# Step 0 of a linear-attention stage in banks of its own, its loads and the first unit after it moved, and settling products of another shape

## The chip, the cores and the metric

The kernel runs on one core of one Trainium2 chip. The metric is the device time of one execution in microseconds (us). Five engines run their own instruction queues side by side: PE (TensorE, matrix products into PSUM), DVE (VectorE), ACT (ScalarE), POOL (GpSimd) and SP (SyncE, which here issues every transfer). An instruction waits on semaphores for what it needs, and everything behind it on its engine waits with it.

## The reference

```python
def _attn_ref(r, k, v, w, u):               # (4, 8, 768, 48): batch, heads, time, width
    state = np.zeros((B, H, D, D))
    for t in range(S):
        kt, vt, rt = (k[:, :, t], v[:, :, t], r[:, :, t])
        cur = np.einsum('bhd,bhe->bhde', u[None] * kt, vt)
        y[:, :, t] = np.einsum('bhd,bhde->bhe', rt, state + cur)
        state = w[None, :, :, None] * state + np.einsum('bhd,bhe->bhde', kt, vt)

def _moe_ref(x, w_gate, w_val, w_out):      # 3072 tokens, 384 -> 1536 -> 384
    gate = 1.0 / (1.0 + np.exp(-(x @ w_gate)))
    return gate * (x @ w_val) @ w_out

def _moe2_ref(x, w_in, w_out):              # 384 -> 2048 -> 384
    h = np.maximum(x @ w_in, 0.0)
    return h * h @ w_out
```

The output is `_moe2_ref(_moe_ref(x))`, where x is y with batch and time as 3072 tokens and heads and width as 384 features.

## The kernel before

**Attention.** Time is cut into six steps of 128 positions (`NCH`), two halves of 64 each. A unit is one step of one of four batches: units 0 to 3 are step 0, units 4 to 7 step 1, and so on to 23. `load_unit` fetches a unit in four transfers (`kv`, `rn`, `kT`, `rT`, 1.1 MB). The recurrence is done in blocks: `attn_pre` (POOL) and `attn_sum` (DVE, into `dv`) give the diagonal of the scores, `attn_diag` (ACT, eight small activations) writes it into `am`; `attn_prep` (DVE) scales kT and rT by decay tables; `attn_scores` (PE) multiplies them into PSUM, and `attn_mask` (DVE) copies the scores under the mask into `am`. `attn_kh` (POOL) scales k, `attn_sums` (PE) makes each half's sum of k by v, and `attn_us` (ACT) copies it out. `attn_mid` and `attn_state` (DVE) carry the state on.

**A visit.** `attn_out(n)` is one visit of PE to attention: the masked scores of unit n by v, the first `reads` of the state, a `settle`, then scores and sums of unit n + 1, a `settle` ahead of and behind the sums, and the second `reads`. ACT then copies `us` of n + 1 and the results `ys`; two transfers (six after the fourth unit) put `ys` into `xraw`, the input x of the next stage. All PSUM of a visit is the tile `att`, three banks: outputs y1 and y2, scores `pa` and sums `pu` lie in halves of them. `settle` is a small product into an unused tile; it stands wherever the products behind it write, from another half of PE's rows, a bank that products ahead of it write.

**Hidden layers.** `phases` lists the stages of the two feed-forward networks: phase 0 is the first seven hidden units (`CUT`) of network 1 on step 0, the next phases are network 1 on steps 1 to 5, then the rest of step 0, then network 2. `inner(i, f, fill)` makes one hidden unit f: nine products `pg`, a sigmoid `s` (ACT), nine products `pv`, `s` times `pv` (DVE), its split into `gh` (ACT) and `gl` (POOL in phase 0, else DVE), and, one unit late, nine products of the projection (`finish`). Each operand is split into a high and a low part, so a product takes three passes.

**Weights.** `convert` turns 64-bit weights into such pairs as a pipeline over three calls: ACT and DVE on `raw`, DVE on the next, ACT (`wu`, high) and POOL (`wu`, low) on the one after. `load_raw` fetches a `raw` tile (0.4 MB), four deep.

**What sets the order.** The program is written in order by hand (`manual_schedule`), each engine taking its instructions in that order. In phase i the attention of step i + 1 is spread over slots, three for each hidden unit (`unit_ops`; `fill` runs a slot's operations, then one `convert`). `starts` says at which slot each unit's visit stands. `warm` puts filler products on PE. The tiles of a pool's tag rotate through `bufs` buffers.

In step 0 (line 631 on) the order of one round is `attn_pre`, `attn_prep` of unit n + 2, fillers, the visit n, `attn_sum(n + 2)`, `attn_mask(n + 1)`, `attn_mid`, `attn_state(n)`, then diagonals and `attn_kh` of n + 2. After the fourth round stand two conversions, 24 fillers and the split of x into `xh` (ACT) and `xl` (DVE).

## Time and profile before

| | us |
|---|---|
| median of three runs (989.1 to 991.38) | 990.55 |
| the profiled execution | 990.49 |
| its span, first to last instruction | 988.7 |
| PE busy in the span | 961.3 |
| DVE, ACT, POOL busy | 453.1, 401.8, 135.0 |
| mean granted clock of PE | 0.976 |

The page's slices cut the span into 40 equal parts of 24.7 us and give each engine's busy share in tenths; `PEclk` is the clock that PE was granted, in tenths of full speed (5 is 1.2 GHz, 9 is the full 2.4). The timeline lists instructions by start: start, length, engine, line, operation, result from operands, count, and in brackets how long the engine was idle before and what ended that. The window views give busy time of each engine, its count in brackets, then granted clock, the DMA engines' mean busy share and GB/s.

### The profile page before, as it was taken

Reading aid. Unit: us, or ns where it says so; the run is one execution under the profiler, and the core shown is the slowest. Engines: PE = TensorE matmul, PEld = TensorE weight load, DVE = VectorE, ACT = ScalarE, POOL = GpSimd, SP = SyncE. Lnnn points to the kernel's source line nnn. Section 1 sums busy time; section 2 is a strip of 40 time slices with the busy share of each in tenths; the row PEclk is TensorE's granted clock in tenths of the full one; section 3 lists DMA queues with packets and bytes.
Section 4 is the critical chain, followed back from the end, with each engine's and each line's share of the span. In section 5 each row is a group of like instructions: output and inputs, shape, how many; then the busy total and the mean of one; then the engine's idle time right before and its main releaser. Section 6 shows DMA issues by size and latency. Waiting matters only on the chain.

```text
span 988.7 us, 16639 instructions
## 1 busy us (share of the span) xinstructions
PE 961.3 (97%) x6904; PEld 764.3 (77%) x6904; DVE 453.1 (46%) x742; ACT 401.8 (41%) x826; POOL 135.0 (14%) x121
## 2 busy tenths in 40 slices
PE   6888899999999999999999999999999999999997
PEld 3566688888888888887888888888888888888886
DVE  5667757754434444422344465343333433433332
ACT  3656756533233223322366564232332322323322
POOL 6446735300000000000033121000000000000000
PEclk7679899999999999999999999999999999999999
DMA  8664555522122221100244440010100100100000
GB/s 302 203 211 126 169 167 161 147 79 84 52 60 89 90 67 27 68 7 15 95 128 123 154 155 1 1 64 1 33 32 1 64 1 1 65 1 1 32 0 33
DMA packets 42235, 76.86 MB, mean 78 GB/s; under 512 B 5168, under 2 KB 17584, under 8 KB 42160
## 3 DMA queue, kind: packets, MB, share of 16 engines
q1 hardware_dynamic: 42160, 75.80, 24.1%
q8 instruction: 54, 0.88, 0.4%
q14 instruction: 21, 0.17, 0.1%
HBM read 60.05 MB, written 11.01 MB: 72 GB/s over the span
## 4 chain that ended last, share of the span: by engine, by line
PE 90%; DVE 4%; ACT 2%; issue 1%; POOL 1%; DMA 1%; SPq 0%; DVEq 0%; ACTq 0%
PE pg L429 34%; PE two L448 16%; PE pv L429 14%; PE po L448 11%; PE att L448 7%; PE att L270 5%; PE pw L590 1%; PE tok L278 1%; DVE first L239 1%; DMA first<-in_rkv 1%; DVE am L319 1%; ACT am L255 1%; POOL wu L134 0%; DVE raw L156 0%; DVE mid L388 0%
## 5 line engine op out<-in xcount | busy, mean ns | idle before, releaser
L429 PE MATMUL pg<-xh,wu 128*128 128x512 f32 x1008 | 315.0, 397 | 5.8 <-ACT wu L133 3.7
L429 PEld LDWEIGHTS pg<-xh,wu 128*128 128x128 f32 x1008 | 189.8, 188 | 54.2 <-ACT wu L133 5.0
L429 PE MATMUL pg<-xl,wu 128*128 128x512 f32 x504 | 195.0, 395 | 0.0
L576 ACT CAST gh<-s 128x512 fp32r<-128x512 f32 (+1 forms) x169 | 104.9, 621 | 194.0 <-DVE s L572 120.6
L412 DVE TENSOR_TENSOR gl<-s,gh 128x512 fp32r<-128x512 f32 x162 | 113.3, 699 | 86.6 <-PE po L448 56.3
L575 DVE TENSOR_TENSOR s<-s 128x512 f32<-128x512 f32 (+1 forms) x97 | 66.6, 687 | 181.4 <-ACT s L574 181.4
L448 PE MATMUL two<-gh,wu 128*128 128x512 f32 x472 | 148.1, 395 | 0.0
L429 PE MATMUL pv<-xh,wu 128*128 128x512 f32 x432 | 141.2, 408 | 0.4 <-POOL wu L134 0.4
L574 ACT ACTIVATE s<-pg 128x512 f32<-128x512 f32 (+1 forms) x97 | 57.6, 594 | 190.3 <-PE pg L429 190.3
L572 DVE TENSOR_TENSOR s<-pv,s 128x512 f32<-128x512 f32 x72 | 49.6, 689 | 176.1 <-PE pv L429 172.6
L429 PEld LDWEIGHTS pg<-xl,wu 128*128 128x128 f32 x504 | 95.0, 189 | 22.7 <-DVE xl L412 0.3
L448 PEld LDWEIGHTS two<-gh,wu 128*128 128x128 f32 x472 | 89.3, 189 | 21.7
L448 PE MATMUL po<-gh,wu 128*128 128x512 f32 (+1 forms) x338 | 105.5, 392 | 0.0
L429 PEld LDWEIGHTS pv<-xh,wu 128*128 128x128 f32 x432 | 81.1, 191 | 21.0 <-POOL wu L134 0.8
L448 PE MATMUL two<-gl,wu 128*128 128x512 f32 x236 | 92.5, 392 | 0.0
L558 ACT ACTIVATE s<-pg 128x512 f32<-128x512 f32 x72 | 43.6, 606 | 110.5 <-PE pg L429 110.2
L429 PE MATMUL pv<-xl,wu 128*128 128x512 f32 x216 | 86.8, 402 | 0.0
L448 PEld LDWEIGHTS po<-gh,wu 128*128 128x128 f32 x338 | 63.4, 188 | 14.6
L154 ACT ACTIVATE raw<-raw 128x384 bf16<-128x384 bf16 x68 | 73.6, 1082 | 0.0
L448 PE MATMUL po<-gl,wu 128*128 128x512 f32 (+1 forms) x169 | 66.2, 392 | 0.0
L448 PE MATMUL att<-gh,wu 128*128 128x512 f32 (+1 forms) x204 | 63.4, 392 | 0.0
L255 ACT ACTIVATE am<-anti,dv 128x64 f32<-128x64 f32 x192 | 50.1, 340 | 16.5 <-DVE dv L245 16.5
(295 smaller groups left out, 919.6 us busy)
## 6 DMA issues: line engine op xcount, KB each, us to landing
raw<-in_w SPq DMA_DIRECT2D x68, 384.0 KB, 3.2
kv<-in_rkv SPq DMA_DIRECT2D x16, 384.0 KB, 3.3
xin<-x2d SPq DMA_DIRECT2D x6, 768.0 KB, 4.2
out<-x2s SPq DMA_DIRECT2D x18, 256.0 KB, 2.0
first<-in_rkv SPq DMA_DIRECT2D x16, 256.0 KB, 5.8
kT<-in_rkv SPq DMA_DIRECT2D x16, 256.0 KB, 4.5
rT<-in_rkv SPq DMA_DIRECT2D x16, 256.0 KB, 5.0
x2d<-x2s SPq DMA_DIRECT2D x15, 256.0 KB, 2.0
```

The source lines that it names most:

```text
L154: nc.scalar.activation(top, top, AF.Prelu, scale=2.0**-112, alpha=2.0**32)
L239: nc.vector.tensor_mul(t, t, two)
L255: nc.scalar.mul(am_t[n][:, h], anti, dv_t[n][:, h : h + 1])
L270: nc.tensor.matmul(out, lhsT=lhsT, rhs=rhs, start=(bank, q) not in opened, stop=True, skip_group_check=True)
L412: (eng or nc.vector).tensor_tensor(out=dst, in0=src, in1=high.bitcast(F32), op=ALU.subtract)
L429: nc.tensor.matmul(ps, lhsT=a, rhs=b_, start=(i == 0), stop=(i == len(pairs) - 1))
L448: nc.tensor.matmul(po[k][:, ts], lhsT=a, rhs=b_[:, ts], start=(first and m == 0), stop=(last and m == 2 and ts is cuts[-1]),)
L558: nc.scalar.activation(s, pg, AF.Sigmoid)
L572: nc.vector.tensor_tensor(out=s[:, ts], in0=pv[:, ts], in1=s[:, ts], op=ALU.mult)
L574: nc.scalar.activation(s[:, ts], pg[:, ts], AF.Relu)
L575: nc.vector.tensor_mul(s[:, ts], s[:, ts], s[:, ts])
L576: nc.scalar.copy(gh[:, ts], s[:, ts])
```

## The change

It has these parts. Scores of units 0 to 3 go to a tile `pa0` of two banks (tag `o`, used by the projection later), and stand ahead of the visit's other products instead of within it. In step 0 the state updates are left out of the rounds and done in `attn_mid` of step 1 (units 5 to 7, and unit 4), for which `us` gets five buffers. Unit 4's scores, sums and `us` stand behind the loop and not in visit 3; unit 5's preparation goes to the first three slots of phase 0. Transfers are put in another order, units 6 and later are fetched from visit 4 on. Table products stand ahead of the first scores. The visits of phase 0 stand at slots 3, 8, 12, 17 (were 0, 3, 9, 12), those of later phases at 0, 9, 18, 27 (were 0, 6, 15, 24). Fillers: 8, 2, 4, 4 and then 4 and 14, were 8, 6, 2, 2 and 24. `settle` loads 48 columns and not 8, so that its product has the shape of the others.

```diff
--- before.py
+++ after.py
@@ -67,7 +67,7 @@
     IN_W = 8
     CUT = 7
 
-    WARM0, WARM_OUT, WARM_X = 13, (8, 6, 2, 2), 24
+    WARM0, WARM_OUT, WARM_X = 13, (8, 2, 4, 4), (4, 14)
 
     anti = cp.tile([C, L], F32, name="anti")
     mask8 = cp.tile([C, L], U8, name="mask8")
@@ -102,6 +102,8 @@
             o += m
         for i in (2, 3, 0, 1):
             nc.sync.dma_start(out=got[i][0], in_=got[i][1])
+            if n == 0 and i == 3:
+                nc.sync.dma_start(out=u_bc, in_=u.to_broadcast([C, H * D]))
         k_t[n], r_t[n] = (t[0:DP].rearrange("p (j t) -> p j t", j=HP) for t, _ in got[:2])
         kv_t[n], rn_t[n] = got[2][0], got[3][0]
 
@@ -207,12 +209,12 @@
             nc.scalar.copy(th.rearrange("p (j r d) -> p j r d", j=HP, r=2)[:, :, par], pth)
 
 
-    am_t, dv_t = {}, {}
+    am_t, dv_t, pa_t = {}, {}, {}
     bank, us_t, mid_t = {}, {}, {}
 
 
     att = pp.tile([P, 3, 512], F32, name="att")
-    pa = att[:, 1:3, 0 : HP * L].rearrange("p r (j t) -> p r j t", j=HP)
+    pas = att[:, 1:3, 0 : HP * L].rearrange("p r (j t) -> p r j t", j=HP)
     y1, y2 = att[:, 0, 0 : HP * L], att[:, 2, HP * L :]
     PU = HP * L
     pu = [att[:, i, PU : PU + HP * D].rearrange("p (j d) -> p j d", j=HP) for i in (1, 0)]
@@ -275,19 +277,26 @@
     def settle(x):
 
         tok = pp.tile([P, T], F32, tag="v", name="tok")
-        nc.tensor.matmul(tok[0:8, 0:8], lhsT=x[0:D, 0:8], rhs=x[0:D, 0:8], start=True, stop=True)
+        nc.tensor.matmul(tok[0:D, 0:8], lhsT=x[0:D, 0:D], rhs=x[0:D, 0:8], start=True, stop=True)
 
     def attn_scores(n):
 
         if n >= NU:
             return
         k, r = k_t[n], r_t[n]
+        banks, pa_t[n] = (1, 2), pas
+        if n < B:
+
+            two = pp.tile([P, 2, T], F32, tag="o", name="pa0")
+            banks, pa_t[n] = (3, 4), two[:, :, 0 : HP * L].rearrange("p r (j t) -> p r j t", j=HP)
+            opened.difference_update([(m, q) for m in banks for q in range(2)])
+        pa = pa_t[n]
         for j in range(HP):
             for par in range(2):
                 x = slice(64 * par, 64 * par + D)
                 for a in range(2):
                     t = slice(a * L, (a + 1) * L)
-                    mm64(1 + par, a, pa[64 * a : 64 * a + L, par, j], k[x, j, t], r[x, j, t])
+                    mm64(banks[par], a, pa[64 * a : 64 * a + L, par, j], k[x, j, t], r[x, j, t])
 
 
     width = (64, D)
@@ -316,13 +325,13 @@
             return
         am = am_t[n].rearrange("p (j r) t -> p r j t", r=2)
         m = mask8.unsqueeze(1).unsqueeze(1).to_broadcast([C, 2, HP, L])
-        nc.vector.copy_predicated(am, m, pa)
+        nc.vector.copy_predicated(am, m, pa_t.pop(n))
 
     def attn_us(n):
 
         if n >= NU:
             return
-        us = us_t[n] = sp.tile([DP, 2, HP, D], F32, tag="us", name="us", bufs=2)
+        us = us_t[n] = sp.tile([DP, 2, HP, D], F32, tag="us", name="us", bufs=5)
         for a in range(1 if units[n][0] == NCH - 1 else 2):
             nc.scalar.copy(us[:, a], pu[a][0:DP])
         if units[n][0] == 0:
@@ -347,6 +356,8 @@
                         st = mid_t[n][o, j] if a else state[o, b, j]
                         mm(a, q, j, D, st, r_t[n][o, j, a * L : (a + 1) * L])
 
+        if n + 1 < B:
+            attn_scores(n + 1)
         for j in range(HP):
             for q in range(2):
                 h = head(q, j)
@@ -355,13 +366,16 @@
                     mm(a, q, j, width[q], kv[x, h * D :][:, : width[q]], am[x, h])
         reads(0)
         settle(kv)
-        attn_scores(n + 1)
-        attn_sums(n + 1)
+        if n >= B:
+            attn_scores(n + 1)
+        if n != B - 1:
+            attn_sums(n + 1)
         settle(kv)
         reads(1)
-        while len(kv_t) <= n + (4 if len(kv_t) < IN_W + 2 else 3) and len(kv_t) < NU:
+        while n >= B and len(kv_t) <= n + (4 if len(kv_t) < IN_W + 2 else 3) and len(kv_t) < NU:
             load_unit(len(kv_t))
-        attn_us(n + 1)
+        if n != B - 1:
+            attn_us(n + 1)
         if b == 0:
             bank["y"] = sp.tile([P, B, HP, C], F32, tag="ys", name="ys", bufs=1)
             xraw[c] = sp.tile([P, KT, B, C], F32, tag="xraw", name="xr", bufs=1)
@@ -383,6 +397,8 @@
 
         if n >= NU or units[n][0] == 0:
             return
+        if units[n][0] == 1:
+            attn_state(n - B)
         mid = mid_t[n] = sp.tile([DP, HP, D], F32, tag="mid", name="mid", bufs=2)
         nc.vector.tensor_mul(mid, state[:, units[n][1]], decay)
         nc.vector.tensor_add(mid, mid, us_t[n][:, 0])
@@ -457,8 +473,13 @@
 
     def unit_ops(c, tiles):
 
-        starts = [b * (tiles - 1) // B for b in range(B)] + [tiles - 1]
+
+        starts = (0, 9, 18, 27, 36) if tiles == F1 else (3, 8, 12, 17, 21)
         slots = [[] for _ in range(3 * tiles)]
+        if c == 1:
+            slots[0].append(lambda: (attn_pre(B + 1), attn_prep(B + 1)))
+            slots[1].append(lambda: (attn_kh(B + 1), attn_sum(B + 1)))
+            slots[2].append(lambda: (attn_diag(B + 1, 0), attn_diag(B + 1, 1)))
         for b in range(B):
             n = c * B + b
             ops = [
@@ -471,7 +492,7 @@
                 lambda n=n: attn_diag(n + 2, 1),
                 lambda n=n: attn_kh(n + 2),
             ]
-            s0, room = 3 * starts[b], 3 * (starts[b + 1] - starts[b])
+            s0, room = starts[b], starts[b + 1] - starts[b]
             for i, op in enumerate(ops):
                 slots[s0 + i * room // len(ops)].append(op)
         return slots
@@ -597,56 +618,72 @@
         nc.sync.dma_start(out=w_sb, in_=wt)
         id_sb = sp.tile([DP, D], F32, tag="ev", name="id_sb", bufs=2)
         maskf = sp.tile([C, L], F32, tag="ev", name="maskf", bufs=2)
+        nc.sync.dma_start(out=id_sb, in_=ident)
         load_unit(0)
-        nc.sync.dma_start(out=u_bc, in_=u.to_broadcast([C, H * D]))
         nc.sync.dma_start(out=anti, in_=antid)
         nc.sync.dma_start(out=maskf, in_=mask)
-        nc.sync.dma_start(out=id_sb, in_=ident)
         load_unit(1)
+        load_unit(2)
         load_raw(0)
+        load_unit(3)
         load_raw(1)
-        for n in range(2, B):
-            load_unit(n)
-            load_raw(n)
+        load_raw(2)
+        load_unit(4)
+        load_raw(3)
         powers = tables()
         attn_pre(0)
         nc.gpsimd.tensor_copy(mask8, maskf)
+        attn_pre(1)
         attn_prep(0)
+        state_tables(*powers)
+        attn_scores(0)
         attn_sum(0)
-        attn_pre(1)
         attn_diag(0, 0)
         attn_diag(0, 1)
-        attn_scores(0)
+        attn_kh(0)
+        attn_kh(1)
         attn_prep(1)
+        attn_mask(0)
         attn_sum(1)
-        state_tables(*powers)
-        attn_mask(0)
         attn_diag(1, 0)
-        attn_diag(1, 1)
-        attn_kh(0)
         attn_sums(0)
         attn_us(0)
-        attn_kh(1)
-        convert()
+        attn_diag(1, 1)
         for n in range(B):
-            attn_pre(n + 2)
-            attn_prep(n + 2)
+            m = n + 2
+            if m < B:
+                attn_pre(m)
+                attn_kh(m)
+                attn_prep(m)
             warm(WARM_OUT[n])
             attn_out(n)
-            attn_sum(n + 2)
-            attn_mask(n + 1)
-            attn_mid(n + 1)
-            attn_state(n)
-            attn_diag(n + 2, 0)
-            attn_diag(n + 2, 1)
-            attn_kh(n + 2)
-            if n == 0:
+            if m <= B:
+                attn_mask(n + 1)
+            if m < B:
+                attn_sum(m)
+                attn_diag(m, 0)
+                attn_diag(m, 1)
+            if n in (1, 2):
                 convert()
-        for _ in range(2):
-            convert()
-        warm(WARM_X)
+
+        load_unit(B + 1)
+        attn_pre(B)
+        attn_kh(B)
+        attn_prep(B)
+        attn_sum(B)
+        attn_diag(B, 0)
+        attn_diag(B, 1)
+        warm(WARM_X[0])
+        attn_scores(B)
+        attn_sums(B)
+        attn_us(B)
+        convert()
+        convert()
+        warm(WARM_X[1])
         for k in range(KT):
             x_from(0, k)
+        attn_mask(B)
+        attn_mid(B)
         for i, (layer, c, f0, f1) in enumerate(phases):
             ops = unit_ops(i + 1, f1 - f0) if i + 1 < NCH else []
             slot = 0
```

On DVE, in step 0, between the first diagonals and the first conversion. `dv` is a unit's diagonal, `am` its score tile, `first` a loaded piece, `us`, `wdec` and `state` belong to the recurrence. Before:

```order
L245 TENSOR_REDUCE dv_361<-first_89 128x8
L319 COPY_PREDICATED am_239<-mask8_70,att_110 128x2x4x64
L397 TENSOR_TENSOR state_77<-us_267,wdec_76 112x192
L398 TENSOR_TENSOR state_77<-state_77,us_267 112x192
L146 SCALAR_TENSOR_TENSOR wt__376<-raw_154 128x384
L156 TENSOR_SCALAR raw_156<-raw_156 128x384
L239 TENSOR_TENSOR first_90<-first_90,trk_74 112x512
L239 TENSOR_TENSOR first_91<-first_91,trk_74 112x512
```

After:

```order
L328 COPY_PREDICATED am_230<-mask8_70,pa0_211 128x2x4x64
L247 TENSOR_REDUCE dv_244<-first_85 128x8
L241 TENSOR_TENSOR first_86<-first_86,trk_74 112x512
L241 TENSOR_TENSOR first_87<-first_87,trk_74 112x512
L328 COPY_PREDICATED am_246<-mask8_70,pa0_290 128x2x4x64
L247 TENSOR_REDUCE dv_363<-first_89 128x8
L241 TENSOR_TENSOR first_90<-first_90,trk_74 112x512
L241 TENSOR_TENSOR first_91<-first_91,trk_74 112x512
L328 COPY_PREDICATED am_365<-mask8_70,pa0_382 128x2x4x64
```

The masks of step 0 read `pa0` and no longer `att`, each stands ahead of the next unit's `dv`, and no state update stands between them.

On PE, the visit of unit 0 in step 0, from its last products by `am` on (`tok` is the `settle`, `first` by `first` the scores, `first` alone the sums). Before:

```order
L270 MATMUL att_110<-am_196,first_80 48x64 x2
L270 MATMUL att_110<-first_79,us_267 48x64 x4
L278 MATMUL tok_306<-first_80 8x8
L270 MATMUL att_110<-first_83,first_82 64x64 x16
L278 MATMUL tok_324<-first_84 8x8
L270 MATMUL att_110<-first_84 64x48 x2
```

After, from the scores of unit 1, which stand first:

```order
L272 MATMUL pa0_290<-first_83,first_82 64x64 x16
L272 MATMUL att_110<-am_230,first_80 64x64 x2
...
L272 MATMUL att_110<-am_230,first_80 48x64 x2
L272 MATMUL att_110<-first_79,us_269 48x64 x4
L280 MATMUL tok_327<-first_80 48x8
L280 MATMUL tok_329<-first_84 48x8
L272 MATMUL att_110<-first_84 64x48 x2
```

The scores have left the place between the two `tok`, and `tok` is 48x8 for 8x8.

On DVE, where step 0 ends and phase 0 begins (`xl` is x's low part, `wt` a weight in conversion). Before:

```order
L412 TENSOR_TENSOR xl_733<-xr_356,xh_732 128x512
L319 COPY_PREDICATED am_668<-mask8_70,att_110 128x2x4x64
L387 TENSOR_TENSOR mid_836<-state_77,wdec_76 112x192
L388 TENSOR_TENSOR mid_836<-mid_836,us_826 112x192
L397 TENSOR_TENSOR state_77<-mid_663,wdec_76 112x192
L398 TENSOR_TENSOR state_77<-state_77,us_649 112x192
L146 SCALAR_TENSOR_TENSOR wt__846<-raw_168 128x384
L156 TENSOR_SCALAR raw_380<-raw_380 128x384
L146 SCALAR_TENSOR_TENSOR wt__855<-raw_380 128x384
```

After:

```order
L428 TENSOR_TENSOR xl_696<-xr_357,xh_695 128x512
L328 COPY_PREDICATED am_600<-mask8_70,att_110 128x2x4x64
L413 TENSOR_TENSOR state_77<-us_269,wdec_76 112x192
L414 TENSOR_TENSOR state_77<-state_77,us_269 112x192
L403 TENSOR_TENSOR mid_702<-state_77,wdec_76 112x192
L404 TENSOR_TENSOR mid_702<-mid_702,us_648 112x192
L241 TENSOR_TENSOR first_98<-first_98,trk_74 112x512
L241 TENSOR_TENSOR first_99<-first_99,trk_74 112x512
L148 SCALAR_TENSOR_TENSOR wt__724<-raw_172 128x384
```

Behind unit 4's mask now stand the state update of unit 0, then unit 4's `mid`, and unit 5's two `attn_prep` products ahead of the conversions.

## Rows read from the trace of the kernel before

**Rows 1.** the page's slices, each a fortieth of the span.

```profile
PE   6888899999999999999999999999999999999997
...
PEclk7679899999999999999999999999999999999999
```

**Rows 2.** windows in step 0, columns in the first line.

```profile
core 0: us, PE busy (x) PEld busy (x) DVE busy (x) ACT busy (x) POOL busy (x), PEclk, DMA share, GB/s
...
10.00:20.00 10.00, 5.21 (x62) 2.85 (x65) 7.93 (x7) 5.28 (x20) 8.18 (x8) 0.54 1.04 388
20.00:30.00 10.00, 7.43 (x244) 5.20 (x232) 7.06 (x11) 5.39 (x19) 6.90 (x6) 0.97 0.62 214
30.00:40.00 10.00, 8.68 (x209) 6.84 (x212) 5.50 (x12) 4.65 (x19) 2.94 (x3) 0.50 0.80 251
```

**Rows 3.** timeline of step 0: start, length, engine, line, operation, result and operands.

```profile
16.73 3.08 PE L590 MATMUL pw<-idle 128*128 128x512 bf16 x8
...
19.74 0.68 PE L270 MATMUL att<-am,first 64*64 64x64 f32 x32
...
22.66 0.54 ACT L327 COPY us<-att 112x192 f32<-112x192 f32 x2 [4.23 <-PE att L270]
...
23.78 0.73 DVE L319 COPY_PREDICATED am<-mask,att 128x512 f32<-128x512 uint8 x1 [2.91 <-ACT ys L370]
...
41.46 7.81 PE L590 MATMUL pw<-idle 128*128 128x512 bf16 x24
41.62 0.54 ACT L327 COPY us<-att 112x192 f32<-112x192 f32 x2 [3.62 <-issue]
...
42.05 0.66 ACT L370 COPY ys<-att 112x256 f32<-112x256 f32 x2
...
42.57 2.03 ACT L255 ACTIVATE am<-anti,dv 128x64 f32<-128x64 f32 x8
...
47.00 1.77 ACT L416 CAST xh<-xr 128x512 fp32r<-128x512 f32 x3
...
49.42 1.64 PE L429 MATMUL pg<-xh,wu 128*128 128x512 f32 x6
```

**Rows 4.** the chain that ended last: start, length, engine, group, line, count.

```profile
134.15 2.10 PE pg L429 x9
```

**Rows 5.** waits of DVE from 16 to 50 us: total, times, longest.

```profile
DVE am L319 <- ACT ys L370: 10.1, 3, 3.6
```

**Rows 6.** windows of phase 0 and of the rest.

```profile
49.40:124.70 75.30, 64.36 (x717) 49.12 (x718) 53.82 (x79) 46.08 (x102) 44.69 (x36) 0.86 0.54 171
124.70:988.70 864.00, 858.89 (x5580) 692.29 (x5578) 368.54 (x614) 330.91 (x644) 64.15 (x54) 1.00 0.19 60
```

**Rows 7.** waits of ACT in phase 0: total, times, longest.

```profile
ACT gh L576 <- DVE s L572: 9.5, 4, 2.8
ACT us L327 <- PE att L270: 7.9, 4, 2.3
ACT am L255 <- DVE dv L245: 6.5, 4, 2.2
```

**Rows 8.** DVE's groups in phase 0: busy, mean ns of one.

```profile
L397 DVE TENSOR_TENSOR state<-mid,wdec 112x192 f32<-112x192 f32 x4 | 1.8, 461 | 0.0
...
L398 DVE TENSOR_TENSOR state<-state,us 112x192 f32<-112x192 f32 x4 | 1.4, 358 | 0.1
```

**Rows 9.** timeline of PE around one settle.

```profile
127.56 0.22 PE L270 MATMUL att<-rT,state 48*48 48x64 f32 x1
127.57 0.21 PE L270 MATMUL att<-rT,mid 48*48 48x64 f32 x1
127.71 0.20 PE L278 MATMUL tok<-kv 48*8 48x8 f32 x2
127.84 0.69 PE L270 MATMUL att<-rT,kT 48*64 48x64 f32 x32
```

**Rows 10.** PE's groups from 125 us on: the settles.

```profile
L278 PE MATMUL tok<-kv 48*8 48x8 f32 x94 | 9.3, 170 | 0.1
```


## The prediction

> **What bounds the kernel now.** I read the page's slices first: TensorE (PE) is full and at full clock from the sixth slice on, and neither ahead of it [rows 1]. The windows by stage then split the 988.7 us of the span. From 124.7 us on PE is busy for 858.9 of 864.0 us at clock 1.00: there only less PE work helps. Ahead of that lie step 0's attention (to 49.4) and phase 0 (49.4 to 124.7), where PE is busy for 64.4 of 75.3 us at a mean clock of 0.86 [rows 6]. The reader is to see two different limits in these 125 us.
>
> In step 0 the limit is a chain through one visit (one `attn_out`) per unit. The first visit runs on PE from 19.74 to 22.66, where the `us` copy that waits for it starts: 2.9 us. The fourth ends at 41.62, so the three between took 6.3 us each [rows 3]. What stretches them is `attn_mask`, which stands idle until `ys` is copied: 10.1 us in three waits [rows 3, 5]. Behind it the granted clock drops to 0.50 for the whole of 30 to 40 us [rows 2]. Then 24 fillers run for 7.81 us, and phase 0 begins at 49.42, 0.65 us after the third cast of x (47.00 + 1.77) [rows 3].
>
> In phase 0 no engine is full. ACT's idle time tells the chain: 9.5 us for `s`, 7.9 for the visits on PE, 6.5 for `dv`, in four waits each [rows 7].
>
> **Step 0.** The scores now go to `pa0`, banks that nothing else uses before the first projection. So scores(n+1) stand ahead of visit n's products, and mask(n+1) needs only them and its diagonals, not the visit's end. What is late next is the visit's own cycle: on PE 2.9 us and 2 or 4 fillers of 0.23 us (512 columns, as the nine products of [rows 4] that take 2.10), so 3.4 to 3.8; on ACT `us` 0.54, `ys` 0.66 and eight diagonals 2.03, together 3.2 [rows 3]. I take 3.6 us from visit to visit.
>
> The first visit hardly moves: unit 1's loads stand as deep in SP's queue as before, and the same eight fillers (16.73 to 19.81) stand ahead of it [rows 3]. The DMA engines are full from 10 to 20 us, at 388 GB/s [rows 2]; unit 2 now comes ahead of two raw tiles of 0.4 MB, so it lands 2 us earlier, and nobody waits for it there; raw tiles are needed only at the first conversion, which now stands two visits later. `u_bc` ahead of kT costs 0.2 MB, 0.5 us, hidden by the wait for unit 1. `id_sb` earlier lets the table products run under the same cover; uncovered, either would cost its 0.5 us. Visits end at 22.4, 26.0, 29.6 and 33.2, against 41.6.
>
> From there to phase 0 ACT sets the pace in both. Before, 47.00 - 41.62 = 5.4 us from the first `us` to x: `us`, `ys`, diagonals, two conversions [rows 3]. Now unit 4's `us` stands in the row in place of unit 3's, so 5.4 again: x at 38.6, its third cast done at 40.4. The two groups of fillers (4 and 14, about 4 us) end before that. The first two products need not wait for the third cast, so I put the start, comparable to 49.4, at 40.0: **9.4 us earlier**. Ends: 11 if ACT's cycle of 3.2 us rules, 4.4 if the clock falls (below).
>
> **Phase 0.** The slots, the conversions and the visits are the same in number. What is added: unit 5's preparation, formerly in step 0. Its eight diagonals are 2.0 us of ACT [rows 3]; its three POOL products stand among the first weights' low parts, under PE's first three product groups. The state updates of units 0 to 3 come too, inside `attn_mid`: four times 0.46 + 0.36 = 3.3 us of DVE between mask and conversion, in the chain [rows 8]. Visit 7 now stands only three product groups ahead of step 1: 6.3 us of PE [rows 4]. x needs, after that visit, `us` and `ys` (1.2), its transfers (47.00 less the end of `ys`, 42.71, so 4.3) and three casts with a sigmoid between (2.4): 7.9, so 1.6 us of new stall. What goes: the waits of diagonals for `dv`, 6.5 us [rows 7], because `attn_sum` now stands a slot or a conversion ahead of them. Sum: 2.0 + 3.3 + 1.6 - 6.5 = **+0.4**. Ends: +6.9 if the even spacing frees nothing, -7.5 if the 7.9 us for visits goes as well. Units 6, 7 and 8 are now loaded together at visit 4, on SP behind four raw tiles that wait for DVE, and `attn_pre(6)` follows a slot later; POOL has `wu` and `gl` queued behind it, for which PE waits. Two `wu` of POOL and a visit's wait on ACT stand ahead, so I cost it at nothing; uncovered it is a landing, 3 to 5 us, still inside the upper end.
>
> **Settles.** In the saturated part 47 settles remain (94 instructions) [rows 10]. The last `reads` start at 127.56 and 127.57, 10 ns apart; `tok` starts 0.14 us later, and the scores 0.13 after `tok` [rows 9]. That is 0.27 us where two instructions at the pace ahead would take 0.03: 0.24 to gain if the gaps come from the change of shape (48x48 to 48x8 and back), nothing if they come from the ordering itself. I take 0.17, nearer to the upper end because the gap stands on both sides of the odd shape, and less than it because the product now loads 48 columns and still orders: 47 x 0.17 = **8.0 us**; ends 0 and 11.3. The Trainium skill's "TensorEngine Tiling (Array Packing)", Key Properties, says that changing the tiling mode, and not only the tile, drains TensorE. By that the whole 11.3 would go and the sum be 970; the gaps agree with a drain, but no run here yet shows the product without one.
>
> The visits of later steps stand at slots 0, 9, 18, 27 for 0, 6, 15, 24. PE has no wait there to lose [rows 6], and the last visit still leaves two hidden units of work for x to arrive: nothing.
>
> **Sum.** The profiled execution took 990.49 us, 1.8 over its span; the median of the runs is 990.55. 990.5 - 9.4 + 0.4 - 8.0 = **973.5**.
>
> **Rivals.** *The clock falls in step 0.* From 20 to 30 it held at 0.97 [rows 2], with eight fillers; now ten are spread over 20 to 33. At 0.50 a visit and its fillers take up to twice as long, some 1.6 us more after ACT's cover, three times: phase 0 starts 5 us later than in my sum, 978.5. For it: from 30 to 40 visits alone did not bring the clock back. Against: the pauses between them go.
> *Settles cost the same*, the gaps being the ordering: 981.5.
> *Phase 0 is shorter*, ACT's waits for visits gone: 965.6.
> *The mask still waits*, so that the change doesn't do what it says: step 0 gains 2 at most, 981. Against it: `pa0` is a tile of its own, and the order puts the scores ahead.
> *Slower: PE stays at half clock in phase 0.* Even visits and unit 5's work leave PE short runs between waits. 64.4 us at 0.86 are 55 at full clock and 111 at 0.50, where 75.3 stood: +35, 1009. It makes the kernel slower once the mean clock there is under 55 / 92.5 = 0.60. For it: phase 0 was at 0.86 already. Against: a PE that is always busy gets its clock back, as the 24 fillers show (0.325 us each, between the two prices of 0.23 and 0.46) [rows 3].
>
> **How the numbers follow.** My forecast (968 to 978) has 0.45, the clock in step 0 0.18, settles unchanged 0.12, a shorter phase 0 0.13, a mask that waits 0.04, half clock in phase 0 0.08. 973.5 is the likeliest case. The range leaves out the last and the far ends of two others: 962 to 985. Within 0.2% (2 us, about what a measurement of this kernel can tell from no change) I put 0.04, out of the last two: faster 0.89, same 0.04, slower 0.07.
>
> **What would show it.** Right: the masks of units 1 to 3 without a wait for `ys`; visits some 3.6 us apart; clock 1.0 from 20 us to phase 0; first `pg` near 40, step 1's near 115; `tok` under 0.1 us from its neighbours. Wrong: clock 0.50 near 30 us, `attn_pre(6)` waiting for a transfer with `wu` behind it, gaps at `tok` unchanged, or PE idle for more than 2 us where step 1 begins.

## The result, and the profile after

The changed kernel takes 978.83 us (median of four runs, 976.91 to 979.93), the kernel before 990.92 beside it. The ratio is 0.9879, 95% interval 0.9858 to 0.9901: **1.2% faster, 12 us.** The forecast was 973.5, its range 962 to 985. The profiled execution of the changed kernel took 979.93 with a span of 978.1, against 988.7 before: 10.6 us less. The stages say where.

I cut both spans at the same two events: the first `pg` (phase 0 begins) and the second product group `pg` of step 1, from which on PE is full in both kernels. First the windows of before with these borders. The columns are the stretch, its length, busy time of PE, PEld, DVE, ACT and POOL (number of instructions in brackets), granted clock, DMA share and GB/s.

```profile
0.00:49.42 49.42, 38.00 (x610) 22.94 (x610) 30.72 (x51) 24.82 (x80) 26.20 (x32) 0.72 0.77 253
49.42:133.99 84.57, 73.65 (x877) 56.52 (x878) 58.65 (x90) 49.32 (x111) 47.92 (x39) 0.88 0.52 165
133.99:988.70 854.71, 849.60 (x5419) 684.88 (x5417) 363.68 (x604) 327.67 (x636) 60.91 (x51) 1.00 0.19 59
```

The same three of the changed kernel:

```profile
0.00:38.06 38.06, 29.62 (x603) 17.58 (x603) 21.23 (x36) 21.95 (x71) 21.04 (x27) 0.87 0.68 229
38.06:131.40 93.34, 75.97 (x877) 58.05 (x878) 66.49 (x101) 52.87 (x121) 49.85 (x41) 0.85 0.61 192
131.40:978.10 846.70, 841.63 (x5419) 681.42 (x5417) 363.11 (x607) 328.09 (x636) 61.52 (x53) 1.00 0.19 59
```

Step 0 is 11.4 us shorter, phase 0 is 8.8 us longer, and the saturated rest is 8.0 us shorter. Of the 19.4 us that two stages gained, phase 0 takes back 8.8. Its length grew by 8.8 and DVE's busy time in it by 7.8, so DVE stands idle there about as long as before (84.57 - 58.65 = 25.9 and 93.34 - 66.49 = 26.9 us). PE does the same products in it; it is busy 2.3 us longer, at a granted clock of 0.85 and not 0.88, and idle 6.5 us longer (84.57 - 73.65 = 10.9 and 93.34 - 75.97 = 17.4 us). The forecast ended phase 0 at step 1's first `pg`, [rows 6]: by that border the loss is 4.5 us (75.3 before, 117.81 - 38.06 = 79.8 now), and 4.3 more lie in the first hidden unit of step 1. There the first `pg` takes 3.7 us where it took 2.2, since a part of its x comes late, PE waits 1.6 us for `attn_kh`, and behind that the granted clock stands at 0.50 from 126 to 129 us.

**Step 0** did what the change says. First the changed kernel's timeline on ACT, with the `us` copies that end the first three visits, and x's casts (start, length, and in brackets the idle time before and what ended it):

```profile
22.17 0.54 ACT L336 COPY us<-att 112x192 f32<-112x192 f32 x2 [4.95 <-PE att L272]
...
25.44 0.54 ACT L336 COPY us<-att 112x192 f32<-112x192 f32 x2 [0.29 <-PE att L272]
...
29.17 0.62 ACT L336 COPY us<-att 112x192 f32<-112x192 f32 x2
...
37.31 1.73 ACT L432 CAST xh<-xr 128x512 fp32r<-128x512 f32 x3
```

Its timeline on DVE, with the masks of units 1 and 3:

```profile
20.38 0.73 DVE L328 COPY_PREDICATED am<-mask,pa 128x512 f32<-128x512 uint8 x1 [2.01 <-PE pa L272]
...
28.50 0.73 DVE L328 COPY_PREDICATED am<-mask,pa 128x512 f32<-128x512 uint8 x1 [1.88 <-ACT am L257]
```

Its windows that answer two rows of [rows 2], the clock behind the busy times:

```profile
20.00:30.00 10.00, 9.47 (x344) 6.83 (x336) 5.70 (x10) 7.54 (x29) 5.52 (x6) 0.99 0.47 158
30.00:40.00 10.00, 8.57 (x142) 4.96 (x143) 6.31 (x13) 8.40 (x22) 2.09 (x2) 1.00 0.57 153
```

The visits stand 3.3 and 3.7 us apart where they stood 6.3 apart [rows 3]; no mask waits for `ys` any more, where three waited 10.1 us [rows 5]; what a mask waits for now is its own diagonals on ACT or its scores. The clock stays at 2.4 GHz from 20 to 40 us, where it was granted 0.50 from 30 to 40.

**The rest** got its 8.0 us from the settles. On PE, the first settle of a visit in the saturated part, from the last of the `reads` to the scores (`tok` is the settle's product):

```profile
146.84 0.22 PE L272 MATMUL att<-rT,state 48*48 48x64 f32 x1
146.84 0.21 PE L272 MATMUL att<-rT,mid 48*48 48x64 f32 x1
146.89 0.17 PE L280 MATMUL tok<-kv 48*48 48x8 f32 x1
146.90 0.28 PE L272 MATMUL att<-rT,kT 48*64 48x64 f32 x3
```

`tok` starts 0.05 us after the last `reads`, where it was 0.14, and the scores 0.01 after `tok`, where it was 0.13 [rows 9].

**Phase 0** has new waits. From the changed kernel's list of waits between 38.06 and 131.40 (what waited, for what: us in total, times, longest):

```profile
ACT gh L597 <- DVE s L593: 18.1, 6, 4.3
DVE am L328 <- ACT ys L384: 8.5, 4, 3.6
...
DVE s L593 <- PE pv L445: 7.5, 1, 7.5
POOL first L232 <- DMA first<-in_rkv: 6.2, 2, 4.4
...
PE att L272 <- POOL first L264: 5.8, 2, 3.9
ACT xh L432 <- DMA xr<-ys: 5.3, 1, 5.3
```

One line of the same list of before, between 49.42 and 133.99:

```profile
DVE am L319 <- ACT ys L370: 16.2, 5, 4.6
```

ACT's four waits of diagonals for `dv` (6.5 us, [rows 7]) are gone from the list, and DVE's masks wait 8.5 us for `ys` where they waited 16.2. New are a wait of DVE for a `pv` of step 1 (7.5), 6.2 us in which POOL's `attn_pre` of units 5 and 6 waits for its loads, and 5.3 in which x of step 1 waits for its transfers; `gh` waits for `s` for 18.1 us, with 9.5 before up to step 1 [rows 7] and 14.4 between the borders used here.

### The profile page after: what moved, and what is told of

Its sections match the earlier page's. It is cut to its first block, busy times and chain, and to the rows that moved or that the text cites. A ratio compares the mean times of both kernels' runs of the same rounds, so it can differ in the third digit from the quotient of the medians.

```text
span 978.1 us, 16626 instructions
## 1 busy us (share of the span) xinstructions
PE 947.2 (97%) x6898; PEld 757.1 (77%) x6898; DVE 450.8 (46%) x742; ACT 402.9 (41%) x826; POOL 132.4 (14%) x121
## 4 chain that ended last, share of the span: by engine, by line
PE 89%; DVE 2%; DMA 2%; POOL 2%; ACT 1%; SPq 1%; issue 1%; DVEq 0%; POOLq 0%; ACTq 0%
PE pg L445 35%; PE two L464 16%; PE pv L445 15%; PE po L464 12%; PE att L464 7%; PE att L272 4%; DMA first<-in_rkv 2%; SPq L104 1%; DMA xr<-ys 0%; POOL wu L136 0%; POOL gl L428 0%; ACT am L257 0%; ACT raw L156 0%; PE pw L611 0%; POOL first L264 0%
## 5 line engine op out<-in xcount | busy, mean ns | idle before, releaser
L445 PE MATMUL pg<-xh,wu 128*128 128x512 f32 x1008 | 318.3, 400 | 6.5 <-ACT wu L135 3.1
L464 PEld LDWEIGHTS two<-gl,wu 128*128 128x128 f32 x236 | 44.2, 187 | 10.0 <-POOL gl L428 0.3
```

The lines of the kernel that those rows point to most:

```text
L445: nc.tensor.matmul(ps, lhsT=a, rhs=b_, start=(i == 0), stop=(i == len(pairs) - 1))
L464: nc.tensor.matmul(po[k][:, ts], lhsT=a, rhs=b_[:, ts], start=(first and m == 0), stop=(last and m == 2 and ts is cuts[-1]),)
```

## The experiments

The theory at this point: the three stages are separate, and what phase 0 lost has several carriers, each with an experiment: the late loads, the layout of its visits, the state updates on DVE, `attn_kh` behind `wu` on POOL, x where step 1 begins. The rival is that phase 0 has a length of its own, whatever stands in it, so that what is taken out of step 0 comes back there. All runs in one table: the median with its ratio to the kernel before (95% interval), and of the profiled execution the three stages, cut at the two events above, with the busy times of DVE and PE in phase 0 and PE's granted clock there. Each ratio is to executions of the kernel before made beside that run, whose medians were 989.2 to 990.9.

| kernel | median us | ratio | step 0 | phase 0 | DVE in phase 0 | PE in phase 0 (clock) | rest |
|---|---|---|---|---|---|---|---|
| before | 990.92 | 1 | 49.4 | 84.6 | 58.7 | 73.7 (0.88) | 854.7 |
| changed | 978.83 | 0.9879 (0.9858 to 0.9901) | 38.1 | 93.3 | 66.5 | 76.0 (0.85) | 846.7 |
| e2_settle_only | 977.40 | 0.9869 (0.9853 to 0.9885) | 45.4 | 85.2 | 58.9 | 70.9 (0.90) | 846.8 |
| e3_old_settle | 987.61 | 0.9976 (0.9966 to 0.9985) | 38.3 | 92.7 | 66.5 | 73.9 (0.89) | 854.7 |
| e1_early_loads | 980.85 | 0.9901 (0.9882 to 0.9920) | 43.2 | 89.8 | 67.3 | 72.5 (0.90) | 846.9 |
| e4_old_phase0 | 981.69 | 0.9917 (0.9900 to 0.9933) | 42.6 | 92.9 | 66.8 | 75.8 (0.85) | 846.8 |
| s1_state_back | 975.04 | 0.9851 (0.9836 to 0.9866) | 38.7 | 87.2 | 62.1 | 70.9 (0.90) | 846.7 |
| s2_kh_early | 975.28 | 0.9858 (0.9830 to 0.9886) | 38.3 | 89.8 | 65.6 | 74.3 (0.87) | 846.8 |
| s3_loads_spread | 979.22 | 0.9900 (0.9878 to 0.9922) | 42.1 | 87.6 | 65.6 | 70.6 (0.90) | 846.9 |
| s4_visits_sooner | 978.92 | 0.9892 (0.9876 to 0.9909) | 36.7 | 92.6 | 65.5 | 73.8 (0.85) | 847.0 |
| u1_scores_in_visit | 980.36 | 0.9910 (0.9890 to 0.9930) | 41.3 | 90.6 | 67.0 | 72.5 (0.91) | 846.7 |
| c1_state_and_kh | 975.82 | 0.9861 (0.9846 to 0.9876) | 39.6 | 89.8 | 61.6 | 73.5 (0.87) | 846.8 |
| c2_and_visits | 974.74 | 0.9855 (0.9837 to 0.9873) | 37.9 | 86.3 | 64.1 | 71.1 (0.90) | 847.6 |
| b1_state_and_visits | 973.76 | 0.9839 (0.9826 to 0.9853) | 38.5 | 87.1 | 60.6 | 69.7 (0.90) | 846.8 |

Step 0's end moves by 1 to 2 us between profiles in which nothing ahead of it differs (36.7 to 38.3 for the changed kernel, s2 and s4), so a stage of one profile is known to about that; the rest repeats within 0.3 us, but for c2. One thing moves phase 0 beside the waits: with the same 877 or 878 instructions PE is busy in it for 69.7 to 76.0 us, 69.7 to 72.5 where the granted clock is 0.90 or 0.91 and 73.5 to 76.0 where it is 0.85 to 0.89. Its idle time there is 14.3 us in e2 and 15.2 to 18.8 in all kernels that carry the moved parts, 17.4 in the changed one.

### The settles: e2 and e3

```diff
-        nc.tensor.matmul(tok[0:8, 0:8], lhsT=x[0:D, 0:8], rhs=x[0:D, 0:8], start=True, stop=True)
+        nc.tensor.matmul(tok[0:D, 0:8], lhsT=x[0:D, 0:D], rhs=x[0:D, 0:8], start=True, stop=True)
```

e2 is this line alone in the kernel before, e3 the changed kernel with this line undone.

> The kernel before with the settle of 48 columns alone, nothing else changed. Theory: the two gaps of 0.13 to 0.14 us around a settle come from the change of shape and mostly go, 47 settles in the saturated part: 8 us less, 982.5 (11.3 less, 979, if the whole gap goes). Rival: the gaps are the ordering itself and stay: 990.5.

> The changed kernel with the old settle of 8 columns, all else as changed. Theory: the shape is worth the same here as in the kernel before: 8 us more, 987, up to 11 more, 990. Rival: the other parts of the change took the gaps away, and the shape is worth nothing: 979.

e2 came out at 977.40, further than the theory's 982.5 and as fast as the whole change; e3, at 987.61, bears out the theory's 987. The windows of e2 in step 0 and in the rest:

```profile
0.00:45.40 45.40, 31.41 (x609) 19.11 (x610) 27.99 (x50) 23.96 (x79) 26.66 (x32) 0.85 0.83 274
...
130.59:977.40 846.81, 841.63 (x5419) 681.41 (x5417) 363.68 (x604) 327.26 (x637) 60.73 (x51) 1.00 0.19 60
```

Its window from 30 to 40 us, which answers the fourth row of [rows 2]:

```profile
30.00:40.00 10.00, 8.79 (x251) 6.43 (x248) 6.80 (x15) 6.67 (x29) 2.94 (x3) 0.83 0.94 310
```

And the rest of e3:

```profile
130.93:985.60 854.67, 849.60 (x5419) 684.86 (x5417) 363.37 (x607) 328.16 (x636) 61.62 (x53) 1.00 0.19 59
```

The rest is 846.8 with the new shape and 854.7 with the old, whichever kernel carries it: these 8.0 us belong to the settles alone, and the visits' new slots in later phases are worth nothing. In the kernel before, step 0 is also 4.0 us shorter with the line: the visits are shorter, and the clock from 30 to 40 us was granted at 0.83 where it was 0.50 [rows 2]. In the changed kernel the line does nothing for step 0 (38.3 and 38.1). That fits that the parts don't add up: the line alone (0.9869) and all the other edits alone (0.9976) would make 0.9845, and together they make 0.9879. What was reordered brings nothing measurable beyond the line: 977.40 without it, 978.83 with it, the intervals of the ratios overlapping. Without the line it is worth 0.24%, some 2 us (e3).

### The layout of phase 0: e4

e4 is e1 (below) with unit 5's preparation ahead of phase 0, and the visits of phase 0 where they stood before:

```diff
-        starts = (0, 9, 18, 27, 36) if tiles == F1 else (3, 8, 12, 17, 21)
+        starts = (0, 9, 18, 27, 36) if tiles == F1 else (0, 3, 9, 12, 18)
...
+        attn_pre(B + 1)
+        attn_prep(B + 1)
+        attn_sum(B + 1)
+        attn_kh(B + 1)
+        attn_diag(B + 1, 0)
+        attn_diag(B + 1, 1)
         for i, (layer, c, f0, f1) in enumerate(phases):
```

> The kernel e1 (early loads) with phase 0 laid out as before: unit 5's preparation stands ahead of phase 0 and not in its first three slots, and the visits of phase 0 stand at slots 0, 3, 9, 12 and the last at 18 and not at 3, 8, 12, 17 and 21; the state updates stay in phase 0, the later phases stay as changed. Theory: the new layout was to free the waits of diagonals for dv and does so, but it costs the stall of x where step 1 begins and more waits for the visits; I expect the two layouts within 3 us of each other, 972 to 978. Rival: the layout is the main cost of phase 0, and the old one is faster than e1 by over 3 us. Second rival: the new layout is what frees phase 0, and the old one is slower than e1 by over 3 us.

981.69 against e1's 980.85: the two layouts are within 3 us of each other, as the theory has it, though both miss its 972 to 978. The layout is not what phase 0 lost; of the two, the new one is the shorter (89.8 in e1, 92.9 here), all of it in PE's busy time at the two clocks (72.5 and 75.8 us). With the old layout ACT waits for `dv` again, 14.2 us in five waits where e1 has none, and the time differs by 0.8: a wait of that size gone is worth little by itself. e4 and e2 have the same layout, and still phase 0 is 92.9 and 85.2 us. Its window in e2:

```profile
45.40:130.59 85.19, 70.85 (x877) 54.63 (x878) 58.90 (x91) 50.35 (x113) 47.42 (x39) 0.90 0.54 164
```

And in e4:

```profile
42.64:135.58 92.94, 75.84 (x878) 57.95 (x878) 66.82 (x101) 52.14 (x121) 49.97 (x41) 0.85 0.49 151
```

The difference in length is 7.8 us, in DVE's work 7.9. That pointed to what was moved into phase 0 on DVE.

### The state updates: s1

```diff
-        if units[n][0] == 1:
-            attn_state(n - B)
...
             if m < B:
                 attn_sum(m)
+            attn_state(n)
+            if m < B:
                 attn_diag(m, 0)
```

> The changed kernel with the state updates of units 0 to 3 back in the rounds of step 0 (behind a unit's dv), none of them in attn_mid of step 1. Theory: DVE's two instructions for each of the four updates lie in the chain of phase 0 (mask, state, mid, conversion), where they take 0.36 to 1.06 us each, and in step 0 DVE waits anyway; step 0 stays within 1 us and phase 0 shortens by 3 to 5 us, 974 to 976. Rival: they are covered by other waits in phase 0, and the time stays within 1 us of 978.8. Second rival: they delay step 0's masks by as much as phase 0 gains.

975.04: 3.8 us less than the changed kernel by the medians, 2.8 by the ratios, whose intervals just overlap; every one of its runs is below every one of the other's. Step 0 holds the four updates at 38.7 us, within what profiles differ there, and phase 0 falls by 6.2 us to 87.2:

```profile
38.68:125.86 87.18, 70.88 (x878) 54.38 (x879) 62.08 (x93) 52.79 (x121) 50.11 (x41) 0.90 0.64 203
```

Of the 6.2 us, 5.1 are PE's busy time, at a clock of 0.90 and not 0.85, and 1.1 its idle time. These profiles are also the fastest of s1's four executions and the slowest of the changed kernel's, so 6.2 is too large a size for the effect. The clock alone doesn't make the gain, though: executions of equal mean clock over the whole span took 974.68, 975.41 and 975.55 us in s1 (0.981, 0.983, 0.983) and 979.60 and 978.06 in the changed kernel (0.981, 0.983). The updates' groups on DVE in phase 0 of the changed kernel (behind the bar busy us and mean ns of one, then idle us before them):

```profile
L414 DVE TENSOR_TENSOR state<-state,us 112x192 f32<-112x192 f32 x8 | 4.9, 616 | 0.3
...
L413 DVE TENSOR_TENSOR state<-us,wdec 112x192 f32<-112x192 f32 x4 | 3.5, 872 | 0.0
...
L413 DVE TENSOR_TENSOR state<-mid,wdec 112x192 f32<-112x192 f32 x4 | 1.6, 407 | 0.0
```

The same in phase 0 of s1:

```profile
L411 DVE TENSOR_TENSOR state<-mid,wdec 112x192 f32<-112x192 f32 x4 | 2.8, 705 | 0.0
L412 DVE TENSOR_TENSOR state<-state,us 112x192 f32<-112x192 f32 x4 | 2.8, 703 | 0.1
```

And in step 0 of s1:

```profile
L411 DVE TENSOR_TENSOR state<-us,wdec 112x192 f32<-112x192 f32 x4 | 2.8, 707 | 0.0
...
L412 DVE TENSOR_TENSOR state<-state,us 112x192 f32<-112x192 f32 x4 | 1.4, 358 | 0.2
```

In phase 0 of the changed kernel state updates take 10.0 us of DVE, in s1's 5.6; the 4.2 us that they take in step 0 cost it some 1 us by the means (37.9 to 39.6 us in the four kernels that have them there, 36.7 to 38.3 in the three whose step 0 is otherwise the same), no more than profiles differ, since DVE waits there anyway. The rival with no effect and the one with a later step 0 both fall. This is the one carrier of phase 0's loss that moving it alone has shown.

### The loads: e1 and s3

In e1 units 5 to 7 are fetched in the opening list, in s3 units 5 and 6 ahead of the visits of units 2 and 3 and unit 7 behind the rounds:

```diff
         load_raw(3)
+        for n in range(B + 1, IN_W):
+            load_unit(n)
...
-        load_unit(B + 1)
         attn_pre(B)
```

```diff
+            if n >= 2:
+                load_unit(B + n - 1)
             warm(WARM_OUT[n])
             attn_out(n)
...
-        load_unit(B + 1)
+        load_unit(B + 3)
```

> The changed kernel with one thing put back: units 5, 6 and 7 are fetched in the opening list of transfers, behind unit 4 and the fourth raw tile, and no longer from the end of step 0 and visit 4 on. Theory: the late loads cost phase 0 several us, because POOL's attn_pre of units 5 and 6 waits for them (6.2 us in two waits in the changed kernel) with wu and gl queued behind it; then the time falls by 3 to 5 us, from 978.8 to about 975, and phase 0 up to the end of unit 8's visit shortens from 87.5 to 83 or 84 us. Rival: those waits lie under others (ACT's for the visits, the weights), and the time stays within 1 us of 978.8.

> The changed kernel with units 5 and 6 fetched ahead of the visits of units 2 and 3, and unit 7 behind the rounds of step 0, so that none of them stands behind x's transfers or behind visit 4, and none ahead of the opening list's end as in e1. Theory: e1 gained 2 us in phase 0 and lost 5 in step 0, where its loads took bandwidth from units 2 to 4; spread out they lose less, 1 us in step 0 and gain 2 to 4 in phase 0: 976 to 978. Rival: every byte ahead of x's own transfers delays x, and the time is that of e1, 981.

Neither gained: 980.85 and 979.22. Phase 0 is shorter by 3.6 and 5.7 us, and step 0 is longer by 5.1 and 4.1. POOL's waits for the loads are gone in both, but PE stands idle in phase 0 as long as before, 17.3 and 17.0 us for 17.4; what fell is its busy time, 72.5 and 70.6 us for 76.0, at a clock of 0.90 and not 0.85. So the runs don't show that the 6.2 us of waiting were what phase 0 lost; b1 below has 7.7 us of them and a phase 0 of 87.1. Step 0 of e1 in its windows:

```profile
0.00:43.18 43.18, 32.15 (x604) 19.34 (x604) 21.79 (x36) 22.25 (x71) 21.43 (x28) 0.80 0.84 289
```

Step 0 of s3:

```profile
0.00:42.12 42.12, 27.35 (x598) 17.43 (x604) 22.33 (x36) 22.13 (x71) 23.33 (x29) 0.84 0.82 269
```

From the list of waits of s3 in step 0, those where x is cast:

```profile
PE pg L445 <- ACT xh L432: 5.7, 1, 5.7
...
ACT xh L432 <- DMA xr<-ys: 4.6, 1, 4.6
```

The DMA engines' share of step 0 goes from 0.68 to 0.84 and 0.82. In s3 the visits end as early as in the changed kernel, and then x's own transfers are late: ACT waits 4.6 us for them, PE 5.7. What phase 0 gains, step 0 loses, to within 2 us. The theory for e1 had a shorter phase 0 right and left out what the same bytes take away in step 0; s3, with the ratio of e1 (0.9900 and 0.9901), bears out its rival.

### `attn_kh` on POOL: s2

```diff
-                lambda n=n: (attn_state(n), attn_pre(n + 2)),
+                lambda n=n: (attn_state(n), attn_pre(n + 2), attn_kh(n + 2)),
...
-                lambda n=n: attn_kh(n + 2),
```

> The changed kernel with one operation of a visit's list moved in all phases: attn_kh of a unit stands right behind its attn_pre on POOL and no longer last, behind the wu and gl that follow. Theory: the visits of phase 0 wait for attn_kh (5.8 us in PE's waits for it there), which stands in POOL's queue behind wu that wait for ACT and DVE; ahead of them it is done in time, phase 0 loses most of the 5.8 us, and the time is 974 to 976. Rival: the wait is only the last of several, wu and gl become later by the same microsecond, and the time stays within 1 us of 978.8.

975.28, 3.5 us less than the changed kernel by the medians; the runs (973.17 to 979.02) overlap with the other's (976.91 to 979.93), and so do the intervals, so that the gain is likely and not shown. The chain of waits of the changed kernel shows what it is about (start, length, what), between the loads of unit 6 and the visit of unit 5:

```profile
53.53 6.11 DMA first<-in_rkv
...
59.70 1.26 POOL first L232
...
62.05 1.07 POOL wu L136
63.12 1.71 POOL gl L428
...
71.20 0.97 POOL first L264
...
72.21 1.09 PE att L272 x28
```

A landing of 6.1 us holds `attn_pre` (L232), behind it stand `wu` and `gl`, and behind those `attn_kh` (L264), for which the visit on PE waits, until 72.2. In s2 PE's waits for `attn_kh` are gone (8.4 us in the changed kernel, 5.8 for the loaded tiles `first` and 2.6 for `kv`), but it waits 13.5 us for weights where it was 5.9. Most of the one wait came back as the other, and phase 0 is 3.6 us shorter in the profile, half of it in PE's busy time (74.3 us for 76.0).

### The visits' slots: s4

```diff
-        starts = (0, 9, 18, 27, 36) if tiles == F1 else (3, 8, 12, 17, 21)
+        starts = (0, 9, 18, 27, 36) if tiles == F1 else (3, 7, 11, 15, 19)
```

> The changed kernel with phase 0's visits at slots 3, 7, 11, 15 and the last of them done by 19, not 3, 8, 12, 17 and 21. Theory: the last visit then stands two thirds of a hidden unit earlier, and the wait for x where step 1 begins (5.3 us on ACT behind the transfers) goes: 974 to 976. Rival: the visits are paced by their own chain through DVE, ACT and POOL, and come no sooner by another slot, or the product groups between them wait instead: within 1 us of 978.8.

978.92, no difference: the rival. The reason is a wait that the slots brought in. PE's longest wait in phase 0 of s4, the first of its list:

```profile
PE tok L280 <- DVE s L593: 6.8, 2, 5.3
```

Slot 7 stands right behind a `pv`. The settle's tile takes turns with `pv` in one bank (both have the tag `v`), so `tok` waits until DVE has multiplied `pv` with `s`. In the changed kernel, whose visits stand ahead of a `pv` or behind a projection, that wait is 1.6 us in two. ACT's wait for x's transfers is gone in s4, but with the new wait beside it the run doesn't price it.

### The scores' place: u1

```diff
-        if n < B:
-            two = pp.tile([P, 2, T], F32, tag="o", name="pa0")
...
-        if n + 1 < B:
-            attn_scores(n + 1)
...
-        if n >= B:
-            attn_scores(n + 1)
         if n != B - 1:
+            attn_scores(n + 1)
             attn_sums(n + 1)
```

> The changed kernel with the scores of units 0 to 3 back in att, between the settles of a visit, as before; loads, fillers, conversions and everything else as changed. Theory: the banks of their own are what shortened step 0, because a mask then waits for nothing that the visit does; without them the masks of units 1 to 3 wait again for ys, some 3 us each, step 0 is 7 to 9 us longer, and phase 0 gives none of it back: 986 to 988. Rival: step 0 gains by the other edits (loads by need, unit 4's scores and unit 5's preparation taken out), and the scores' place is worth under 3 us. Second rival: step 0 is longer by 7 to 9 us but phase 0 shorter by as much, because it waits for weights and loads at a time of their own: within 2 us of 978.8.

980.36, so the theory falls. The masks do wait for `ys` again, in step 0 of u1:

```profile
DVE am L323 <- ACT ys L376: 8.1, 3, 4.1
```

But step 0 is longer by 3.2 us only, with the clock granted at 1.00 from 20 to 40 us, and phase 0 is shorter by 2.8. The first rival stands. Of the 11.4 us by which step 0 shrank, the banks of their own bring some 3, and e3 has 11.1 without the new settles, though e2 got 4.0 from them in the old order. The rest must come from the other edits (loads by need, conversions later, less in the rounds); no run takes these apart.

### Together: c1, c2 and b1

c1 is s1 and s2 together. c2 is c1 with the visits at slots `(3, 8, 12, 15, 18)`. b1 is c2 with `attn_kh` back at the list's end, that is, s1 and those slots.

> s1 and s2 together: state updates back in step 0, attn_kh right behind attn_pre. Theory: they lie on different engines' queues and at different places of the chain (DVE behind the mask, POOL ahead of a visit), and their gains of 3.8 and 3.5 us add up: 971 to 972.5. Rival: they shorten the same wait of PE for a visit, and together bring no more than s1 alone: 974 to 975.

> c1 with phase 0's visits at slots 3, 8, 12 and 15, the list of the last one spread to slot 18. In s4 a visit at slot 7 stood right behind pv, and its settle, which shares pv's bank, waited for DVE's product with s (6.8 us in two waits); here only slot 8 keeps its place. Theory: the wait for x where step 1 begins (5.3 us in the changed kernel) mostly goes, 2 to 4 us less than c1. Rival: as in s4 the visits come no sooner by an earlier slot and something else waits: within 1 us of c1.

> c2 with attn_kh back at the end of a visit's list: the changed kernel with the state updates back in step 0 and phase 0's visits at slots 3, 8, 12, 15, the last one's list ending at slot 18. Theory: in c1 and c2 attn_kh ahead of wu and gl makes PE wait for wu instead (7.1 and 3.6 us in c2 where the changed kernel had under 2), so its gain in s2 is not to be had beside the state's; without it the time is 972 to 974, 1 to 2 less than c2 and about 2 less than s1. Rival: the visits wait for attn_kh again and lose 1 to 3 us against c2: 976 to 978.

c1, 975.82, is nearer to its rival: the gains of s1 and s2 don't add up. That both shorten one chain through POOL, DVE and PE is likely, and not shown. c2, 974.74, is 1.1 better by medians, inside its rival's 1 us as far as these runs can tell. PE's waits in its phase 0 begin with:

```profile
PE pg L443 <- POOL wu L136: 7.1, 4, 2.4
PE pv L443 <- POOL wu L136: 3.6, 4, 1.9
```

That is the price of an early `attn_kh`, 10.7 us of waiting for `wu` where the changed kernel has 2.8. **b1, without it, has the lowest median: 973.76 (971.92 to 975.00), ratio 0.9839, interval 0.9826 to 0.9853**, inside its theory's 972 to 974. The interval is clear of the changed kernel's, and overlaps with those of s1 and c2. PE does wait for `attn_kh` again, 7.6 us, as the rival said, at no loss. Its phase 0:

```profile
38.52:125.61 87.09, 69.73 (x877) 54.38 (x878) 60.56 (x93) 52.45 (x121) 48.65 (x41) 0.90 0.63 202
```

No engine waits for x's transfers at step 1 in b1's list, where ACT in s1 waits 5.6 us, and phase 0 is still 87.1, where s1 had 87.2: taking the stall at the boundary away brought nothing there (PE is idle for 17.4 us, 16.3 in s1).

## Why the prediction was right, and where it was not

The result was inside the range of 962 to 985 and just above the 968 to 978 that had most of the weight; the forecast was 5.3 us too low. The three terms, in the profiled execution: −9.4, +0.4, −8.0 predicted; −11.4, +8.8, −8.0 measured, where the second is +4.5 by the forecast's own border, the first `pg` of step 1, and the forecast had no term for the 4.3 behind it. So the sum had one term right in size, and it gave the reordering 9.0 us (9.4 less 0.4), of which e3 shows 2.

**Settles: right, in size too.** 47 × 0.17 was 8.0; measured 854.71 − 846.70 = 8.0, over the 44 settles that lie in that stretch, 0.18 each of the 0.24 that were to gain. The bound of 11.3 was by all of it. The Trainium skill, "TensorEngine Tiling (Array Packing)", Key Properties, has the mode switch drain the engine; e2 and e3 agree with that in kind: a product of the others' shape in the same place leaves 0.06 of 0.27 us ahead of the first scores. What the forecast left out is that the same line shortens step 0 by 4.0 us in the old order (e2).

**Step 0: right in what it names, 2 us too small.** Visits came 3.3 and 3.7 us apart (3.6 forecast), the clock held, the masks lost their wait. x was cast at 37.3, not 38.6, and the first `pg` stood 0.75 us behind it, not 1.4. The rivals of a falling clock and of masks that still wait did not happen. But the reason given first, the mask behind `ys`, is worth 3 us of it (u1), not most.

**Phase 0: the step that failed.** The sum 2.0 + 3.3 + 1.6 − 6.5 is wrong in three terms. The state updates were priced at 0.46 + 0.36 from their mean in before [rows 8]; here they took up to 1.06 us each, so that the four that were moved make 6.3 us of DVE (3.5 of L413, 2.8 of the 4.9 of L414) and not 3.3. s1 gained 3 to 4 us by taking them out. Unit 5's preparation was priced by its ACT and POOL instructions; its two products with the decay table (2.4 us from 42.73 on) and its `dv` (0.5) are DVE's as well. And the 6.5 us of waits for `dv`, which did go, were counted as a gain of time. DVE's idle time in phase 0 stayed at 26 us, where its masks wait less for `ys` and it waits more for `pv`; in e4 the waits for `dv` are back, and its time is 0.8 us longer than e1's. So the wait was mostly replaced by others. The step costed at nothing, `attn_pre(6)` behind late loads with `wu` behind it, showed as 6.2 us of waiting, and this sign was named ahead. What it costs phase 0 is open (e1, s3), and it is not to be had back, since the loads cost as much in step 0. The stall of x at step 1 was forecast at 1.6 and is a wait of 5.3 on ACT, behind which PE waits 1.0 for `s`.

The upper end of +6.9 let the even spacing free nothing, but had no term for DVE's further work, and none for what lies behind step 1's first `pg`. That the miss is 5 us and not 7 is luck, since step 0 erred by 2.0 the other way; the range of 962 to 985, wide for other reasons, would have held either way. The rival of half clock in phase 0 didn't come true (0.85 against 0.88), nor the one of a shorter phase 0.

**The net.** What is left open: which part of phase 0's loss beyond the state updates belongs to the loads, to unit 5, to the stall at step 1 and to the clock. e1, s3, s4 and c2 each removed a wait and got another, or the same idle time of PE at another clock; none of them settles it. The clock may be no cause by itself: in the changed kernel it is granted 0.50 from 48 to 54, 72 to 78 and 90 to 94 us, each time behind a stretch in which PE stood nearly idle (busy for 0.0, 0.3 and 0.0 of the 2 us from 44, 70 and 86 on). No run holds it while it changes the waits. That phase 0 is DVE's work and some 26 us more (25 to 28) fits nine of the fourteen kernels in the table; in e1, s2, s3, u1 and c2 DVE waits 22 to 24. That is an observation, not a mechanism.

## What to carry to other kernels

Price a move into a stage by all the engines that it loads there, and give a wait that disappears no gain unless the engine that was waited for does less: count what the busiest in-order queue of that stage gets to do. Before a stage of one profile is compared with that of another, split its length into PE's busy and idle time: a different granted clock moves the first with the same work. When a change has many parts, run the smallest alone first; here one line gave as much as all of them together. Work that is moved out of a stage in which its engine waits anyway can cost its full price where it lands without such cover.
